# A new order table for a fused attention and two-layer kernel, and 48 casts of its gated layer given to another engine

## The chip, the cores and the metric

The kernel runs on one core of a Trainium2 chip. The core has a matrix engine (TensorE, PE below), a vector engine (VectorE, DVE), a scalar engine (ScalarE, ACT), a third elementwise engine (GpSimd, POOL) and a sync engine (SyncE, SP) that here only issues transfers. Each works through its own queue of instructions in order and waits at semaphores for the others; PE writes its results into PSUM, the others read them there. The metric is the device time of one launch in microseconds, as a median over several runs.

## The reference

Three layers one behind the other. The first is an attention with a state that is corrected at each of 768 steps; the second is gated, with an RMS norm ahead of it; the third has one activation, h·tanh(softplus(h)).

```python
k_n = k / (np.linalg.norm(k, axis=-1, keepdims=True) + 1e-06)   # B=4, H=8, S=768, D=48
for t in range(S):
    kt, vt, bt = (k_n[:, :, t], v[:, :, t], beta[:, :, t, None])
    y[:, :, t] = np.einsum('bhd,bhde->bhe', q[:, :, t], state)
    v_old = np.einsum('bhde,bhd->bhe', state, kt)
    state = state + bt[:, :, :, None] * np.einsum('bhd,bhe->bhde', kt, vt - v_old)
x = np.ascontiguousarray(y.transpose(0, 2, 1, 3)).reshape(B * S, H * D)     # 3072 x 384
xn = x / np.sqrt(np.mean(x * x, axis=-1, keepdims=True) + 1e-06) * rms_g
g = xn @ w_gate                                                            # 384 x 1536
x = (g * (1.0 / (1.0 + np.exp(-g))) * (xn @ w_val)) @ w_out                # 1536 x 384
h = x @ w_in2                                                              # 384 x 2048
out = (h * np.tanh(np.log1p(np.exp(h)))) @ w_out2                          # 2048 x 384
```

## The kernel before

**Numbers in two halves.** All products of the two layers are made from a high half that PE reads at its fast rate and a low half with the rest, in three matmuls (high·high, high·low, low·high). So each operand needs a cast that makes the high half and a subtraction that makes the low one. The weights come as 64-bit numbers and are first put together on DVE, 128x384 at a time, in `value`: L268 (ACT) or L270 (DVE), then L272, L275, L280 and L283 (DVE); after it the high half L305 (ACT) or L307 (DVE) and the low half L308 (DVE or POOL). L357 is the cast of the same kind for the third layer's weights.

**Phase one: attention, with part of the gated layer beside it.** The 768 steps are 12 rows of 64. A row turns its `q` and `k` (transposes L789 on PE, copied out by L790 on ACT), makes the scores `p` (L769 on PE, masked by L779 on DVE into `PT`), the values (L1163, copied by L1168 on ACT into `ve`), the part that comes from the state (L1138), the outputs (L1181, copied by L1189) and the update of the state (L1214 on PE, added by L1219 on DVE). Ahead of that a triangular 64x64 system is inverted for each head and row. The first four rows use a short form of this, the "quick lane": L938 to L1005 on DVE make the blocks `N`, `X` and `A` in 16x16 pieces, and L1023 on PE multiplies them up, with L1028 on DVE (`Zq`) between two of the multiplications. L690 on DVE normalises a row's `kh`. From row 2 on, a first part of the gated layer (two of six blocks of its hidden width) runs beside the rows: up products L421 to L423, SiLU L473, down products L455 to L457, whose sums are copied by L1303 (`par`) on ACT or DVE and stored. L1242, L1245 and L1252 make a row's two halves of the layer's input.

**Phase two** (`phase_b2`, `gated_pairs`) computes the remaining four blocks for 6 pairs of rows. A unit is nine matmuls of 512 columns for `pg`, nine for `pv` (L1461 to L1463, tile `pu` in the profile), and nine down products L1474 to L1476. Between them ACT makes the SiLU `sg` (L1484), DVE multiplies it by `pv` (L1487) and casts the product to its high half `hh` (L1490), and POOL subtracts for the low half `hl` (L1491). A unit's down products are issued two units later (`LG`=2). Beside the units run the conversions of the third layer's weights and, in `forms_of`, sums and halves of the layer's finished output (L1561 on ACT, L1562 on POOL, L1574 on DVE).

**Phase three** is the third layer, almost all matmul.

**What sets the order.** The work is written as Python generators. Two functions decide whose next piece is issued: `plan` takes for each stream a list of due times and always advances the stream with the earliest one, and `merge` shares out by cost. All their numbers stand in one table `P`: `ROW0`, `ROW1`, `QP`, `L`, `K1` to `K4`, `S`, `T`, `G`, `CV` are due times of the first four rows' streams and of the weight conversions; `R0` to `R11` are the order of the steps in each row (`q0 q1` the turning of q, `p` the scores, `r` the residual, `v` the values, `y` the part from the state, `o0 o1` the outputs, `k` the state's update, and so on); `DUE`, `CVS`, `LR`, `C` are amounts and costs for `merge`. The due times order the program text alone; the chip goes by queues and semaphores. Further entries pick an engine: `XDR` and `PDR` say for each row whether L1245 and L1303 are on DVE (1) or ACT (0), `BAV` and `BLV` whether the high half of a weight of the remaining blocks is made on ACT (1) or DVE, and whether its low half is made on DVE (1) or POOL.

Of the kernel before, what the change touches and what calls it, by code (L numbers as in the profile page):

```python
# [19 lines left out]
P = dict(  # L20
    LN0=0.527,
    LNT=(101.823, 0.05),
    FAV=[0, 1, 1, 0, 0, 0],
    XDR=[0, 0, 0, 0, 0, 0, 0, 1, 0, 1, 0, 1],
    PDR=[0, 0, 0, 0, 0, 1, 0, 0, 0, 0, 0, 1],
    BLV=[0, 0, 0, 0, 0, 1, 0, 0, 1, 1, 0, 1],
    BAV=[0, 1, 1, 1, 1, 1, 1, 0, 0, 0, 1, 1],
    CB=[12.0, 12.0],
    PF=[5.192, 30.818, 9.175, 4.627, -31.291],
# [27 lines left out]
    R6="nA q0 q1 S r nB T y v p X Y k o0 c0 c1 g o1".split(),
    R7="r q0 nA q1 S p nB T v y X Y c0 o0 c1 o1 k g".split(),
    R8="r nA q0 S T q1 p X y nB v Y c1 o0 g c0 k o1".split(),
    R9="r nA q0 S q1 nB T p X c1 y v k g Y c0 o0 o1".split(),  # L60
    R10="r q0 q1 p S y X T v o0 Y o1 k".split(),
    R11="S r q0 q1 p T y X Y v o0 k o1".split(),
    DUE=[-20.443, 5.84, 4.881, 10.56, 10.883, 10.311, 10.883, 10.566, 8.191, 10.779, 10.857, 11.898],
    CVS=[-0.332, 18.493, 8.167, -23.236, 9.058, -3.972, 15.147, -22.515, -14.058, -35.503, -28.424, -8.878],
    LR=[-10.2, 25.182, 19.094, 12.02, 16.416, 13.382, 22.451, 16.703, 20.252, 19.685, 56.75, 78.665],
    C={'n': 0.225, 'q': 0.5, 'r': 1.4, 'y': 1.1, 'p': 1.2, 'v': 1.2, 'o': 0.9, 'k': 1.38, 's': 0.168, 'x': 0.595,
        'c': 0.4, 'd': 0.167, 'g': 1.02, 'h': 1.357},
    ROW0=[23.019, 25.696, 30.249, 44.915, 45.626, 49.289, 21.158, 3.409, 52.039, 52.631, 54.162, 59.926, 14.374,
        44.933, 77.944],
    ROW1=[53.942, 35.537, 46.444, 56.274, 50.209, 32.154, 23.865, 62.891, 61.444, 37.535, 36.083, 60.421, 59.815,  # L70
        70.152, 81.857, 92.68, 97.453],
# [1777 lines left out]
```

## Time and profile before

| | |
|---|---|
| median of 3 runs | 1129.47 us (1128.81 to 1129.47) |
| the profiled execution, its time | 1129.23 us |
| the profiled execution, its span | 1127.5 us |
| busy: PE, DVE, ACT, POOL | 1064.6, 826.8, 498.8, 451.1 us |
| mean granted clock of PE | 0.966 of full speed |

The span runs from the first to the last instruction that the profiler recorded; the time of the execution is a little longer. The busy times are those of one execution. An engine's busy time says how much work it has, its idle time says nothing until one sees what waits for it: time is lost only where the chain of work that ends last stands still.

### The profile page before, as it was taken

The numbers are of one execution on the slowest core, as the hardware profiler recorded it, in microseconds if no ns is written. First come the engines' busy times: TensorE is split into PE (matmuls) and PEld (weight loads), VectorE is DVE, ScalarE is ACT, GpSimd is POOL, SyncE is SP. The second block draws the span as 40 slices with busy tenths as digits, with TensorE's granted clock in tenths as the row PEclk, the third lists the DMA queues.
The fourth block names the chain that finished last, engine by engine and source line by source line (L and its number), as shares of the span: only waits on it lengthen the run. The fifth ranks groups of instructions, "written<-read, shape, count | busy, mean of one in ns | idle before, by whom it ended". The sixth has DMA issues, their size and how long they took to land.

```text
span 1127.5 us, 31819 instructions
## 1 busy us (share of the span) xinstructions
PE 1064.6 (94%) x13146; PEld 970.4 (86%) x13146; DVE 826.8 (73%) x1609; ACT 498.8 (44%) x1076; POOL 451.1 (40%) x435
## 2 busy tenths in 40 slices
PE   5778689999999998999999899999999999999997
PEld 5767679999899897888888678889999999999997
DVE  7668898777888889878979983466765656565662
ACT  4475547686657733233333332234433333343333
POOL 2031234443223442466667665534433333333332
PEclk8686799999999999999999999999999999999999
DMA  9033323333236556267769878754735363542621
GB/s 169 7 74 88 101 58 88 87 87 90 56 85 204 181 169 205 75 219 236 244 231 343 277 262 311 267 204 146 249 112 184 94 219 85 165 153 84 207 69 30
DMA packets 178496, 175.18 MB, mean 155 GB/s; under 512 B 84624, under 2 KB 153232, under 8 KB 178352
## 3 DMA queue, kind: packets, MB, share of 16 engines
q1 hardware_dynamic: 169712, 159.00, 46.3%
q10 hardware_dynamic: 8640, 14.16, 3.8%
q8 instruction: 103, 1.69, 0.6%
q14 instruction: 41, 0.34, 0.1%
HBM read 114.53 MB, written 58.59 MB: 154 GB/s over the span
## 4 chain that ended last, share of the span: by engine, by line
PE 79%; DVE 10%; ACT 5%; issue 3%; DMA 2%; SPq 1%; POOL 0%; ACTq 0%; POOLq 0%; DVEq 0%
PE pd L1474 7%; PE pd L1679 6%; PE pd L1678 6%; PE pd L1677 6%; PE ph L1720 5%; PE ph L1721 5%; PE ph L1722 5%; PE pu L1461 4%; PE pu L1463 4%; PE pu L1462 4%; PE pp L769 2%; PE pp L1023 2%; PE pg L421 2%; PE pd L455 2%; PE pp L1181 2%
## 5 line engine op out<-in xcount | busy, mean ns | idle before, releaser
L1667 POOL TENSOR_TENSOR gl<-t,gh 128x512 fp32r<-128x512 f32 x96 | 124.1, 1294 | 244.8 <-ACT gh L1666 201.1
L1729 DVE TENSOR_TENSOR ou<-ou,ph 128x256 f32<-128x256 f32 x210 | 88.4, 421 | 121.8 <-ACT ou L1727 71.9
L1655 ACT ACTIVATE t<-t 128x512 f32<-128x512 f32 x96 | 60.9, 634 | 185.9 <-DVE t L1729 181.0
L1491 POOL TENSOR_TENSOR hl<-sg,hh 128x512 fp32r<-128x512 f32 x48 | 65.8, 1370 | 79.2 <-DVE hh L1490 78.8
L1677 PE MATMUL pd<-wqh,gh 128*128 128x384 f32 x288 | 97.4, 338 | 0.0
L1679 PE MATMUL pd<-wqh,gl 128*128 128x384 f32 x288 | 97.2, 338 | 0.0
L1678 PE MATMUL pd<-wql,gh 128*128 128x384 f32 x288 | 97.2, 338 | 0.0
L483 POOL TENSOR_TENSOR hl<-sg,hh 128x512 fp32r<-128x512 f32 x24 | 34.5, 1437 | 84.9 <-DVE hh L482 50.6
L1487 DVE TENSOR_TENSOR sg<-sg,pu 128x512 f32<-128x512 f32 x48 | 32.7, 681 | 47.4 <-PE pu L1463 32.0
L283 DVE SCALAR_TENSOR_TENSOR t<-raw,t 128x384 int32<-128x384 int32 x68 | 60.6, 892 | 2.4
L1666 ACT CAST gh<-t 128x512 fp32r<-128x512 f32 x96 | 59.5, 621 | 3.9
L1562 POOL TENSOR_TENSOR fx<-xu,fx 128x256 fp32r<-128x256 f32 x60 | 49.9, 839 | 17.4 <-ACT fx L1561 16.4
L1677 PEld LDWEIGHTS pd<-wqh,gh 128*128 128x128 f32 x288 | 54.5, 189 | 0.0
L1678 PEld LDWEIGHTS pd<-wql,gh 128*128 128x128 f32 x288 | 54.4, 189 | 0.0
L1679 PEld LDWEIGHTS pd<-wqh,gl 128*128 128x128 f32 x288 | 54.0, 188 | 0.4 <-POOL gl L1667 0.4
L1484 ACT ACTIVATE sg<-pu 128x512 f32<-128x512 f32 x48 | 28.5, 594 | 49.1 <-PE pu L1463 47.8
L280 DVE SCALAR_TENSOR_TENSOR t<-raw,t 128x384 int32<-128x384 int32 x68 | 46.6, 685 | 1.4
L421 PE MATMUL pg<-XP,wgh 128*128 128x256 f32 x144 | 45.5, 316 | 0.0
L1561 ACT CAST fx<-xu 128x256 fp32r<-128x256 f32 x60 | 23.4, 402 | 49.6 <-DMA xf_d<-fx 27.1
L421 PE MATMUL pv<-XP,wvh 128*128 128x256 f32 x144 | 44.9, 312 | 0.0
L275 DVE TENSOR_SCALAR t<-t 128x384 int32<-128x384 int32 x68 | 42.7, 627 | 2.3
L455 PE MATMUL pd<-hh,woh 128*128 128x256 f32 x132 | 39.8, 301 | 2.3 <-ACT par L1303 2.2
(331 smaller groups left out, 3619.0 us busy)
## 6 DMA issues: line engine op xcount, KB each, us to landing
xf_d<-fx SPq DMA_DIRECT2D x96, 256.0 KB, 3.1
wr<-wi_d SPq DMA_DIRECT2D x120, 192.0 KB, 2.6
XG<-xf_d SPq DMA_DIRECT2D x40, 384.0 KB, 4.5
raw<-in_moe_w_out_dram SPq DMA_DIRECT2D x28, 384.0 KB, 3.9
wi_d<-ws SPq DMA_DIRECT2D x20, 384.0 KB, 3.2
XP<-xf_d SPq DMA_DIRECT2D x20, 384.0 KB, 6.1
raw<-in_moe_w_in_dram SPq DMA_DIRECT2D x16, 384.0 KB, 3.9
wq_d<-ws SPq DMA_DIRECT2D x16, 384.0 KB, 4.1
```

The costliest lines, as they stand in the source:

```text
L283: nc.vector.scalar_tensor_tensor(out=ti, in0=low, scalar=29, in1=ti, op0=ALU.logical_shift_right, op1=ALU.bitwise_or)
L421: nc.tensor.matmul(ps[:, f, :], wh[:, kt, sl], xh[:, kt, :], start=(kt == 0), stop=False)
L455: nc.tensor.matmul(ps, wh[:, f, sl], hh[:, f, :], start=(i + f == 0), stop=False)
L1474: nc.tensor.matmul(ps, w[:, f, cols_of[o]], h, start=first and i == 0, stop=last and i == 2)
L1491: nc.gpsimd.tensor_tensor(out=hl, in0=sg, in1=hh.bitcast(F32), op=ALU.subtract)
L1655: nc.scalar.activation(out=t, in_=t, func=ACTF.Mish)
L1666: nc.scalar.copy(gh, t)
L1667: nc.gpsimd.tensor_tensor(out=gl, in0=t, in1=gh.bitcast(F32), op=ALU.subtract)
L1677: nc.tensor.matmul(ps, gh, wh, start=(f == fs[0]), stop=False)
L1678: nc.tensor.matmul(ps, gh, wl, start=False, stop=False)
L1679: nc.tensor.matmul(ps, gl, wh, start=False, stop=last)
L1729: nc.vector.tensor_tensor(out=at(to), in0=at(a), in1=at(b), op=PLUS[sign])
```

## The change

The table `P` gets new numbers nearly throughout, and three options are added. Two of them (`HC`, which would move the casts of the first part of the gated layer, and `DG`, another way to take diagonal blocks) are zero everywhere and change nothing in the program. The third, `HB`, is 1: the 48 casts of L1490 are issued on ACT. The core of the diff:

```diff
-    XDR=[0, 0, 0, 0, 0, 0, 0, 1, 0, 1, 0, 1],
-    PDR=[0, 0, 0, 0, 0, 1, 0, 0, 0, 0, 0, 1],
-    BLV=[0, 0, 0, 0, 0, 1, 0, 0, 1, 1, 0, 1],
-    BAV=[0, 1, 1, 1, 1, 1, 1, 0, 0, 0, 1, 1],
+    XDR=[0, 0, 0, 0, 0, 0, 0, 0, 0, 1, 0, 1],
+    PDR=[0, 0, 0, 0, 0, 0, 0, 0, 0, 0, 0, 0],
+    BLV=[1, 0, 0, 0, 0, 1, 0, 1, 0, 1, 1, 1],
+    BAV=[0, 1, 1, 1, 1, 1, 1, 0, 1, 0, 0, 1],
...
-    R1="r nA q0 q1 y v p o0 o1 s0 s1 nB k x0 c0 c1 g".split(),
+    R1="r nA q0 q1 p v y o0 nB o1 s1 s0 k x0 c0 c1 g".split(),
...
+    HC=[0] * 24,
+    DG=[0] * 6,
+    HB=1,
...
-                    nc.vector.tensor_copy(hh, sg)
+                    nc.scalar.copy(hh, sg) if P["HB"] else nc.vector.tensor_copy(hh, sg)
                     nc.gpsimd.tensor_tensor(out=hl, in0=sg, in1=hh.bitcast(F32), op=ALU.subtract)
```

In numbers of instructions: PE issues the same matmuls. From DVE go the 48 casts, six products L1245 (row 7) and six copies L1303 (rows 5 and 11); ACT gets the casts, the copies, and six instances of L1252 with two subtractions on POOL in the place of the products. Of the 12 weights of the remaining blocks three have their low half moved from POOL to DVE and one from DVE to POOL, and one high half each is moved from ACT to DVE and from DVE to ACT. On PE the order of phases two and three is unchanged; that of phase one changes in places, of which two are shown. The lines of the changed kernel have numbers that are higher by 6 (L769, L789) or 10 (L1023 and above).

The first place is PE's queue for row 0, at about 20 to 40 us of the profile. `qp` is row 0's q, `kh_185` and `kh_186` are the k of rows 2 and 3, and the matmuls into `p_558` and `p_559` (64 in all, of which the first stand here) are row 0's scores. Before:

```order
L769 MATMUL pp<-kT_189 64x64 x32
L789 MATMUL pp<-ident,qp 128x128 x8
L789 MATMUL pp<-ident,kh_185 128x128 x8
L769 MATMUL pp<-kT_190 64x64 x32
L769 MATMUL p_558<-QT,kT_188 64x64
L769 MATMUL p_559<-QT,kT_188 64x64
...
L789 MATMUL pp<-ident,kh_186 128x128 x8
L769 MATMUL pp<-kT_191 64x64 x32
L662 MATMUL pp<-bnat,sel 128x192 x4
L1023 MATMUL pp<-A_194,N__178 32x32 x64
```

and after, where the scores go to `p_484` and `p_485`:

```order
L775 MATMUL pp<-kT_189 64x64 x32
L795 MATMUL pp<-ident,qp 128x128 x8
L775 MATMUL p_484<-QT,kT_188 64x64
L775 MATMUL p_485<-QT,kT_188 64x64
...
L795 MATMUL pp<-ident,kh_185 128x128 x8
L775 MATMUL pp<-kT_190 64x64 x32
L795 MATMUL pp<-ident,kh_186 128x128 x8
L775 MATMUL pp<-kT_191 64x64 x32
L668 MATMUL pp<-bnat,sel 128x192 x4
L1033 MATMUL pp<-A_194,N__178 32x32 x64
```

The scores (now L775) have moved from behind the transposes and products of `kh_185` to ahead of them.

The second place is PE's queue for row 1, at about 74 to 88 us. The matmuls `pp<-QT,kT_189` are row 1's scores, `pp<-v,A_192` (L1163) its values, `pp<-sx,QT` (L1138) the part from the state, and `pp<-A_194,N__178` (L1023) the first product of the next quick lane. Before:

```order
L789 MATMUL pp<-ident,qp 128x128 x4
L1138 MATMUL pp<-sx,QT 64x48 x32
L1163 MATMUL pp<-v,A_192 64x48 x32
L769 MATMUL pp<-QT,kT_189 64x64 x32
L1239 MATMUL pp<-ident,po 128x128 x3
L789 MATMUL pp<-ident,kh_187 128x128 x8
L1181 MATMUL pp<-ve_196,PT 64x96 x8
L1181 MATMUL pp<-ve_197,PT 64x96 x8
L1214 MATMUL pp<-ve_196,kh_184 64x48 x16
L1214 MATMUL pp<-ve_197,kh_184 64x48 x16
L1023 MATMUL pp<-A_194,N__178 32x32 x64
```

and after:

```order
L795 MATMUL pp<-ident,qp 128x128 x4
L775 MATMUL pp<-QT,kT_189 64x64 x32
L1173 MATMUL pp<-v,A_192 64x48 x32
L1148 MATMUL pp<-sx,QT 64x48 x32
L1191 MATMUL pp<-ve_196,PT 64x96 x8
L795 MATMUL pp<-ident,kh_187 128x128 x8
L1249 MATMUL pp<-ident,po 128x128 x3
L1191 MATMUL pp<-ve_197,PT 64x96 x8
L1224 MATMUL pp<-ve_196,kh_184 64x48 x16
L1224 MATMUL pp<-ve_197,kh_184 64x48 x16
L1033 MATMUL pp<-A_194,N__178 32x32 x64
```

The scores have moved ahead of L1163 and L1138, which have changed places with each other, and the first outputs L1181 (now L1191) stand ahead of the transposes of `kh_187`.

The third place is ACT's queue in phase two, at about 636 to 650 us: `sg<-pu` is a unit's SiLU, `ws<-t` and `t<-raw` are the last and the first step of a weight's conversion, `fx<-xu` is the high half of an output sum. Before:

```order
L357 CAST ws<-t 128x384
L268 ACTIVATE t<-raw 128x384
L1561 CAST fx<-xu 128x256 x2
L1484 ACTIVATE sg<-pu 128x512
L357 CAST ws<-t 128x384
L268 ACTIVATE t<-raw 128x384
L357 CAST ws<-t 128x384
L268 ACTIVATE t<-raw 128x384
L1484 ACTIVATE sg<-pu 128x512
```

and after, in which L1500 is the cast that was L1490 on DVE:

```order
L360 CAST ws<-t 128x384
L271 ACTIVATE t<-raw 128x384
L1571 CAST fx<-xu 128x256 x2
L1494 ACTIVATE sg<-pu 128x512
L360 CAST ws<-t 128x384
L271 ACTIVATE t<-raw 128x384
L1500 CAST hh<-sg 128x512
L360 CAST ws<-t 128x384
L271 ACTIVATE t<-raw 128x384
L1494 ACTIVATE sg<-pu 128x512
L360 CAST ws<-t 128x384
```

Behind each SiLU, with one or two steps of a conversion between, there now stands a cast that reads what DVE has made of that SiLU.

## Rows read from the trace of the kernel before

**Rows 1.** The page of the kernel before: busy time of an engine, and the chain of waits by engine.

```profile
PE 1064.6 (94%) x13146; PEld 970.4 (86%) x13146; DVE 826.8 (73%) x1609; ACT 498.8 (44%) x1076; POOL 451.1 (40%) x435
...
PE 79%; DVE 10%; ACT 5%; issue 3%; DMA 2%; SPq 1%; POOL 0%; ACTq 0%; POOLq 0%; DVEq 0%
```

**Rows 2.** Busy time of each engine by stretch of the span (x instructions), clock, DMA share.

```profile
0.00:150.00 150.00, 107.73 (x3253) 98.17 (x3253) 113.04 (x248) 81.60 (x169) 29.94 (x46) 0.77 0.39 83
125.00:150.00 25.00, 14.36 (x322) 12.92 (x320) 24.26 (x52) 10.52 (x23) 9.32 (x9) 0.84 0.25 73
150.00:420.00 270.00, 264.11 (x5934) 245.64 (x5931) 227.87 (x374) 172.52 (x411) 105.55 (x105) 1.00 0.41 112
590.00:655.00 65.00, 60.95 (x252) 47.70 (x252) 63.55 (x90) 21.71 (x51) 41.98 (x39) 0.97 0.90 310
650.00:654.00 4.00, 4.00 (x13) 3.09 (x12) 3.90 (x8) 0.00 (x0) 1.28 (x1) 0.57 0.93 355
```

**Rows 3.** Timeline of PE, 20 to 45 us: start, duration, instruction, [idle time ended by].

```profile
29.81 1.94 PE L789 MATMUL pp<-ident,kh 128*128 128x128 f32 x8 [7.48 <-issue]
...
35.27 1.93 PE L769 MATMUL p<-QT,kT 64*64 64x64 f32 x64
...
41.89 1.29 PE L1023 MATMUL pp<-A,N__178 32*32 32x32 f32 x128
```

**Rows 4.** PE's waits, 590 to 655 us: us in total, times, longest.

```profile
PE pu L1461 <- DVE sg L1487: 2.2, 3, 1.5
PE pu L1461 <- ACT sg L1484: 1.9, 1, 1.9
```

**Rows 5.** Timeline of DVE, 25 to 45 us.

```profile
26.00 0.93 DVE L690 TENSOR_TENSOR kh<-kh,rn 128x768 f32<-128x768 f32 x1
...
28.76 0.95 DVE L690 TENSOR_TENSOR kh<-kh,rn 128x768 f32<-128x768 f32 x1
...
37.11 1.06 DVE L997 STREAM_TRANSPOSE A<-e 128x512 f32<-128x512 f32 x1
...
38.73 1.09 DVE L1005 STREAM_TRANSPOSE A<-e 128x512 f32<-128x512 f32 x1
43.23 0.69 DVE L1028 TENSOR_TENSOR Zq<-pp,qc 128x512 f32<-128x512 f32 x1 [3.41 <-PE pp L1023]
```

**Rows 6.** Timeline of ACT, 24 to 30 us.

```profile
24.93 1.05 ACT L790 COPY QT<-pp 128x512 f32<-128x512 f32 x2
```

**Rows 7.** Timeline of ACT, around 118 and around 649 us.

```profile
118.36 1.28 ACT L473 ACT_TABLE_LOAD   x1
...
120.15 1.01 ACT L268 ACTIVATE t<-raw 128x384 f32<-128x384 f32 x2
...
648.05 0.51 ACT L357 CAST ws<-t 128x384 fp32r<-128x384 f32 x1 [3.02 <-DVE t L283]
...
648.92 0.57 ACT L1484 ACTIVATE sg<-pu 128x512 f32<-128x512 f32 x1
```

**Rows 8.** Timeline of PE, 73 to 92 us.

```profile
76.90 0.68 PE L1138 MATMUL pp<-sx,QT 64*64 64x48 f32 x32 [0.99 <-ACT QT L790]
...
79.58 1.16 PE L769 MATMUL pp<-QT,kT 64*64 64x64 f32 x62 [0.95 <-ACT ve L1168]
```

**Rows 9.** Timeline of DVE, 79 to 122 us.

```profile
80.77 1.29 DVE L779 TENSOR_TENSOR PT<-pp,mpos 128x512 f32<-128x512 f32 x2 [5.39 <-PE pp L769]
...
120.73 0.36 DVE L272 TENSOR_SCALAR t<-t 128x384 f32<-128x384 f32 x1 [4.48 <-ACT t L268]
```

**Rows 10.** DVE by line, 595 to 655 us: xcount, busy us, mean ns.

```profile
L283 DVE SCALAR_TENSOR_TENSOR t<-raw,t 128x384 int32<-128x384 int32 x13 | 13.5, 1040 | 0.5
...
L1490 DVE CAST hh<-sg 128x512 fp32r<-128x512 f32 x8 | 3.9, 490 | 0.3
```

**Rows 11.** The page's costliest groups: out<-in, xcount, busy us, mean ns.

```profile
L1666 ACT CAST gh<-t 128x512 fp32r<-128x512 f32 x96 | 59.5, 621 | 3.9
```

**Rows 12.** The casts L1490, 580 to 660 us: ns minimum/median/maximum, first and last start.

```profile
L1490 DVE CAST hh<-sg x11: 426/428/743, 584.7 to 659.4; 128x512 fp32r<-128x512 f32 x11
```

More of the change, by code (lines that the diff above doesn't have):

```diff
@@ L33 @@
     TB=4,
-    LANE=17.902,
+    LANE=17.897,
     AFTER=6.2,
-    LD=2.543,
+    LD=2.702,
     CVT=9.0,
@@ L57 @@
[L57 to L71, printed above, removed]
@@ L84 @@
-    T=[8.74, 12.356, 29.899, 32.334],
-    G=[11.07, 18.231, 4.585, -15.646],
+    R4="r nA q0 T q1 p nB S y X v Y c0 o0 k c1 g o1".split(),
+    R5="r nA q0 q1 p T y nB S X v Y c0 c1 o0 k g o1".split(),
+    R6="nA q0 q1 nB S r T y v X p Y k o0 c0 c1 o1 g".split(),
+    R7="r q0 nA q1 S p nB T v y X Y c0 o0 c1 k o1 g".split(),
+    R8="r nA q0 S T q1 p v X y nB Y c1 o0 g c0 k o1".split(),
+    R9="r nA q0 S nB q1 c1 T p X v y g k Y c0 o0 o1".split(),
+    R10="q0 q1 p r S y X T v o0 Y o1 k".split(),
@@ new lines @@
+    R11="S r q0 q1 p v y T X k Y o0 o1".split(),
+    DUE=[-6.851, 5.84, 4.881, 10.56, 10.883, 10.311, 10.883, 10.495, 8.203, 10.605, 10.869, 11.93],
+    CVS=[-0.332, 18.493, 8.167, -24.65, -27.037, -37.657, -19.515, -61.539, -49.205, -70.165, -63.379, -8.878],
+    LR=[-10.2, 21.494, 19.043, 13.937, 16.019, 13.048, 23.207, 16.774, 19.804, 20.824, 55.053, 74.744],
+    C={'n': 0.225, 'q': 0.5, 'r': 1.4, 'y': 1.1, 'p': 1.2, 'v': 1.2, 'o': 0.9, 'k': 1.587, 's': 0.168, 'x': 0.595,
+        'c': 0.4, 'd': 0.167, 'g': 1.02, 'h': 1.764},
@@ new lines @@
+    HC=[0] * 24,
+    DG=[0] * 6,
+    HB=1,
+    ROW0=[23.019, 26.028, 23.493, 44.915, 45.859, 49.073, 21.158, 3.409, 52.039, 51.821, 54.259, 59.926, 31.574,
+        43.397, 76.837],
+    ROW1=[53.942, 35.214, 44.06, 56.274, 52.678, 31.783, 22.846, 58.857, 60.716, 36.807, 34.879, 59.293, 35.217,
+        69.214, 81.129, 91.952, 97.453],
+    QP=[[37.124, 37.449, 35.748, 26.234, 23.907], [46.104, 51.045, 20.325, 47.994, 56.112], [63.368, 49.928, 66.42,
+        69.011, 48.635], [74.927, 88.149, 76.965, 73.06, 70.769]],
@@ L86 @@
+    L=[(19.303, 1.152), (44.964, 1.232)],
+    FF=(81.706, 4.376),
+    CV=[37.876, 19.543, 17.064, 72.572, 60.58, 54.136, 28.254, 62.88, 46.414, 76.003, 58.797, 81.358, 73.271,
[3 rows of a table added]
+    K1=[-29.982, 6.362, -15.835, -17.448],
+    K23=[12.043, 13.762, -6.978, 13.741],
+    K4=[45.886, 48.426, 50.474, 37.537],
+    S=[-2.222, 10.628, 22.942, 22.571, 54.472],
+    T=[8.662, 12.356, 28.463, 30.886],
+    G=[11.07, 16.354, -0.054, -18.915],
     BL=33.889,
@@ L481, in gated @@
                 hl = hp.tile([128, 2, T], F32R, tag="hl", name="hl")
-                nc.vector.tensor_copy(hh, sg)
+                if P["HC"][n * FA + m] if pairs[0] == 0 else 1:
+                    nc.scalar.copy(hh, sg)
+                else:
+                    nc.vector.tensor_copy(hh, sg)
                 nc.gpsimd.tensor_tensor(out=hl, in0=sg, in1=hh.bitcast(F32), op=ALU.subtract)
@@ L791, in turn, with diagonal @@
             done.add(key)
-        def diagonal(dst, A):
+        def diagonal(dst, A, sg):
+            if P["DG"][sg]:
+                nc.scalar.copy(dst, A[:, :, 0:32])
+                for o in (32, 96):
+                    nc.scalar.copy(dst[o:o + 32], A[o:o + 32, :, 32:64])
+                return
             nc.scalar.activation(out=dst, in_=A[:, :, 0:32], func=ACTF.Copy, scale=h0[:, 0:1])
@@ L926, in quick_lane @@
             comp = kp.tile([128, 32, 32], F32, tag="X11", name="compq")
-            diagonal(comp, A)
+            diagonal(comp, A, sg)
             for o in (32, 96):
```

23 lines of the change are left out of this document (6 added, 17 removed), and 6 rows, old and new, of the table CV.

## The prediction

> **What bounds the kernel now.** Three views, from coarse to fine. The page first [rows 1]: TensorE (PE) is busy for 1064.6 of 1127.5 us, and the chain of work that ended last is PE for 79%, DVE for 10%, ACT for 5%. So time is to be had only in the 62.9 us where PE idles, or where its clock is low. The table by stretch shows where that is [rows 2]: of the first 150 us PE is busy 107.73, so 42.3 of the idle time lie there, at a mean granted clock of 0.77; from 150 to 420 it idles 5.9 us of 270, and from 590 to 655 4.05 of 65, which leaves 10.7 for all the rest. There are thus two places: the start, where the attention's chains run from PE to DVE and ACT and back, and the short stretch 590–655, where DVE is busy 63.55 of 65 us. The waits come third. At the start the longest is one of 7.48 us before the transposes L789 [rows 3]; in 590–655 PE waits only for the release of `pu` tiles by L1487 on DVE (2.2 us) and by the SiLU L1484 on ACT (1.9 us) [rows 4].
>
> The profiled execution took 1129.23 us, its span 1127.5, so 1.7 us lie around the span and stay; the median of the three runs is 1129.47, 0.24 above it. I work against 1129.23 and add the 0.24 at the end. A change within 0.2% (2.3 us) I call no difference.
>
> **The first place, around 30 us.** PE stands still for 7.48 us until 29.81, because the next thing in its queue is the transposes of `kh_185`, and the DVE multiplication L690 that normalises it runs at 28.76–29.71, as the second of two [rows 3, 5]. The 64 score matmuls of row 0 (1.93 us at 35.27) stand behind them, although they need only `QT`, which ACT copies from 24.93 to 25.98 [rows 3, 6]. The change puts the scores ahead and both L690 next to each other. The scores then run in the idle time, from 26.0 to 27.9; the second L690 ends at 26.00 + 0.93 + 0.95 = 27.9; the transposes start near 28.0, 1.8 us earlier. PE's way from there to L1023 took 41.89 − 29.81 = 12.1 us, of which 1.9 of scores are gone: L1023 could start at 28.0 + 10.2 = 38.2. It also needs `A` of L997, which ends at 37.11 + 1.06 = 38.17: the same time. What is late next is DVE: its Zq (L1028, 43.23, after 3.41 of idling) follows L1005, which ends at 39.82 [rows 5]; L1023's first group, 1.29 us long, ends earlier, at 39.5. The gain at Zq is 43.23 − 39.82 = 3.4. I take **3.3**, and as the low end 1.8, the earlier start of the transposes alone. Two ACT steps L268, which stood in ACT's idle time at 25.9, now stand before the row's `ve` copies; of their 1.0 us (the pair of [rows 7]) I count **0.3** as lost.
>
> **The second place, around 78 us.** Row 1's scores stand behind two groups of matmuls, L1138 and L1163, and their bulk starts at 79.58 [rows 8]. DVE idles 5.39 us for them before L779, and its whole sequence from L779 to Zq hangs on that [rows 9]. The change issues the scores first. They then start with `QT`, for which L1138 waits until 76.90 now [rows 8]; their 1.16 us end near 78.1, and L779, the first of whose two parts needs half of them, can start at about 77.6: 3.2 us earlier than 80.77. Against the full 3.2 stands that `ve`, L1163 and L1138 now come after the scores, and that the state's update L1219, moved forward on DVE by two instructions, waits for what follows them on PE. I take **2.7**; ends 1.0 and 3.2.
>
> **The third place, 96–121 us.** DVE stands still for 4.48 us until 120.73, waiting for the first step of a weight conversion, L268 on ACT, which is queued behind a table load of 1.28 us and a SiLU [rows 7, 9]. The change puts load and SiLU five ACT instructions earlier, ahead of copies that wait for PE anyway. L268 then comes up to 1.28 us plus the SiLU's time earlier. On the other side a Zq that PE waits for goes behind two conversions on DVE, and PE is given nine matmuls of the gated layer to fill that; about 0.6 of the gain may go. Net **0.7**; ends 0 and 1.5. Sum for the start: 3.3 + 2.7 + 0.7 − 0.3 = **6.4**, between 2.5 and 7.8.
>
> **Rows 2 to 11 of the attention, 150–420.** PE idles 5.9 us in all there, so new orders can gain little. What leaves DVE here (six products L1245, six copies L1303) lands on ACT, and DVE has 270 − 227.87 = 42 us of idle time, ACT 97 [rows 2]; that room hides it on either engine. I take 0, ends −2 and +2 (a third of the idle time either way). Likewise 0 for the weights' low halves that change between POOL and DVE, and the high halves that change between DVE and ACT.
>
> **The gated layer's second part.** 48 casts `hh` leave DVE for ACT. In 590–655 they cost DVE 3.9 us (8 at a mean of 490 ns), and DVE is the engine without room there [rows 2, 10]. PE's waits come because DVE falls behind unit by unit; with 2.0 us of casts gone by the first of the two long waits and 3.4 by the second (4 and 7 casts of 0.49), the waits of 1.5 and 1.9 us [rows 4] have lost their cause, and I leave 0.65 of the 4.05: a gain of 3.4, after which PE itself is the limit there. Right behind the wait of 1.9 us the granted clock in 650–654 is 0.57, so mostly the lower of its two levels, 1.2 GHz [rows 2]; 4 us at 0.57 do the work of 2.3, and 1.7 are lost. If the wait goes the dip may go, but one dip proves no cause: I count 1.0. Together **4.4**, ends 2.0 (DVE's waits go, ACT's stays) and 5.7 (all).
>
> On ACT a cast costs 0.62 us, by L1666 of the same size [rows 11]: 48 × 0.62 = 30 us in all, and in 590–655 8 × 0.62 = 5 us, where ACT is busy 21.71 of 65 [rows 2]. What costs is not the time but the queue. The cast waits for L1487 on DVE, and behind it stand L357, L268, the `fx` casts and the next SiLU. From one unit to the next it is (659.4 − 584.7) / 10 = 7.5 us [rows 12]; the subtraction L1491 behind the cast is needed two units later, so 0.62 − 0.43 = 0.2 us more for it lies under 15 us. The next L268 is held by 0.62 us and what is left of L1487; DVE works longer than that on the conversion before it (one L283 takes 1.04 us there [rows 10], one of four steps). So I count nothing, and make the other answer a rival.
>
> **Sum.** 1129.23 − 6.4 − 4.4 = 1118.4, with 0.24 **1118.7 us**. By the low ends of both terms it is 1125.0, and 2 more for rows 2 to 11; by the high ends 1116.0, and 2 less.
>
> **Rivals.** A: the start pays nothing. DVE is busy 24.26 of 25 us in 125–150 [rows 2]; if that stretch starts no earlier because its conversions wait for ACT or for their weights, all that was won before is given back, and only the cast pays: 1129.5 − 4.4 = 1125.1. For it speaks the wait of 4.48 us for L268; against it, that DVE is idle for 150 − 113 = 37 us at the start, in chains that get shorter.
>
> B: the cast pays nothing, since POOL takes the freed DVE time. The casts there take 428 ns at the median, 490 on the mean and up to 743 [rows 10, 12], so something holds DVE up beside its own work. If POOL's subtraction L1491, now behind ACT, holds up each unit's conversion by 0.49 us more than today, the 3.9 us are spent: 1129.5 − 6.4 = 1123.1. The Trainium skill ("SBUF — State Buffer", section "Who interferes with whom") says why it may: a DVE copy within SBUF, and a DVE step with two SBUF inputs, use one port pair with GpSimd, and whichever comes second is blocked for the whole instruction. By that rule the cast's own conflict goes and the subtraction's merely falls on another DVE step; at its worst that gives 1123.1, where the rows' price gives 1118.7, and no row here separates the two.
>
> C, slower: ACT's queue. The wait of 1.9 us arises because the SiLU at 648.92 stands behind an L357 that had itself waited 3.02 us for DVE's L283 [rows 7]. A cast that waits for DVE is one more link of that kind, in every unit. If each of the 11 units from 585 to 660 stalled PE by 1.9 us, they would lose 20.9 where 4.05 are lost now: 1129.5 − 6.4 + 16.9 = 1140. The result is slower from a mean stall of (4.05 + 6.4 + 2.3) / 11 = 1.2 us per unit. Against it: with the same L357 ahead of the SiLUs today, only one such wait occurs in this stretch.
>
> D: nothing measurable, because rows 2 to 11 give back what the start wins and the cast pays its low end: within 2.3 us of 1129.5.
>
> **Chances.** Both pay as summed (1113 to 1122): 0.52. A 0.17, B 0.12, D 0.11, C and anything else slower 0.08. A and B lie below the 0.2% mark, so faster is 0.52 + 0.17 + 0.12 = 0.81, same 0.11, slower 0.08. The range 1112 to 1126.5 holds the sum with its bounds, A and B: 0.81. The likeliest case alone has 1113 to 1122.
>
> **What would show it.** Right: the wait before L789 near 28 us shrinks from 7.5 to about 2, L1028 at 43.23 moves to about 39.9 and L779 at 80.77 to about 74.6, PE idles about 36 us in the first 150, and in 590–655 PE's waits for `pu` are under 1 us, with no dip of the clock behind them. Wrong in the first step: these places are earlier but the rows at 150 us are not (A). Wrong in the second: DVE is still busy 97% there with a longer L283 (B), or the wait is for ACT's `sg` (C). Wrong as a whole: PE idles more than 8 us in 150–420, where its 264 busy us leave no room for a worse order.

## The result, and the profile after

The changed kernel takes 1117.87 us (median of four runs, 1113.8 to 1118.62) where the one before took 1129.47 beside it: a ratio of 0.9891, with a 95% interval from 0.9871 to 0.9911. In a second comparison, with more runs of the kernel before, it was 0.9899 [0.9885, 0.9914]. That is 11 to 12 us, and 1118.7 us was predicted.

The profiled execution of the changed kernel is the fastest of its four, 1113.8 us with a span of 1112.1. About 2.5 us of what it is ahead of the others was won before anything had been moved (below, the last section), so its rows are read against the repeat (span 1119.4) wherever a difference of that size counts. Line numbers are higher by 3 up to L484, by 6 from there to L796 and by 10 from L805 on; so a weight's high half on ACT, L305, is L308 in the changed kernel, and its low half, L308, is L311. The page first, as in [rows 1], with the moved cast beside it:

```profile
PE 1061.1 (95%) x13146; PEld 969.4 (87%) x13146; DVE 787.8 (71%) x1553; ACT 528.7 (48%) x1136; POOL 451.5 (41%) x433
...
PE 81%; ACT 7%; DVE 5%; issue 3%; SPq 2%; POOL 1%; DMA 1%; ACTq 0%; DVEq 0%; POOLq 0%
...
L1500 ACT CAST hh<-sg 128x512 fp32r<-128x512 f32 x48 | 29.8, 621 | 79.4 <-DVE sg L1497 79.4
```

DVE has lost 39 us of work and ACT has gained 30, of which the cast is 29.8, at 621 ns a piece: the price of [rows 11] to the nanosecond. The chain of waits has half as much of DVE (5% for 10%) and more of ACT (7% for 5%). By stretch, with the columns of [rows 2]; 575 to 645 are the same units as 590 to 655 and a few more:

```profile
0.00:150.00 150.00, 117.14 (x3501) 106.75 (x3502) 122.17 (x264) 86.84 (x183) 34.07 (x50) 0.80 0.39 88
125.00:150.00 25.00, 18.73 (x472) 16.79 (x469) 23.57 (x55) 9.18 (x22) 6.35 (x7) 0.86 0.35 78
150.00:420.00 270.00, 263.66 (x5757) 245.73 (x5757) 224.90 (x368) 173.77 (x415) 102.55 (x101) 1.00 0.42 118
575.00:645.00 70.00, 70.00 (x303) 56.51 (x302) 65.63 (x91) 32.57 (x72) 50.09 (x46) 1.00 0.92 313
```

At the start PE now idles 32.9 us instead of 42.3 (36.5 in the repeat); from 150 to 420 it idles 6.3 instead of 5.9; and in the stretch of phase two it does not idle at all, where it had lost 4.05. In the repeat it still idles 1.3 of the 70 us there, in one wait for ACT's SiLU, at a granted clock of 1.00.

The first place, PE and then DVE, as in [rows 3] and [rows 5]:

```profile
23.62 1.41 PE L775 MATMUL p<-QT,kT 64*64 64x64 f32 x64 [3.18 <-ACT QT L796]
25.98 1.94 PE L795 MATMUL pp<-ident,kh 128*128 128x128 f32 x8 [0.95 <-issue]
...
32.43 1.18 PE L775 MATMUL pp<-kT 64*64 64x64 f32 x64 [0.88 <-ACT kT L796]
...
36.36 1.28 PE L1033 MATMUL pp<-A,N__178 32*32 32x32 f32 x128 [1.26 <-DVE A L1007]
```

```profile
24.10 1.78 DVE L696 TENSOR_TENSOR kh<-kh,rn 128x768 f32<-128x768 f32 x2
...
35.18 1.04 DVE L1007 STREAM_TRANSPOSE A<-e 128x512 f32<-128x512 f32 x1
...
36.77 1.08 DVE L1015 STREAM_TRANSPOSE A<-e 128x512 f32<-128x512 f32 x1
37.75 0.65 DVE L1038 TENSOR_TENSOR Zq<-pp,qc 128x512 f32<-128x512 f32 x1
```

The one wait of 7.48 us has become four smaller ones: 3.18 for `QT` ahead of the scores, 0.95 ahead of the transposes, 0.88 for a `kT` copy and 1.26 for `A` of L1007. Zq (L1038) stands at 37.75, right behind L1015, which is what the prediction named as late next; it had put Zq at 39.9 and row 1's mask at 74.6, and the repeat has them at 40.9 and 75.41. The second and third place on DVE, as in [rows 9]:

```profile
72.14 1.29 DVE L785 TENSOR_TENSOR PT<-pp,mpos 128x512 f32<-128x512 f32 x2 [1.39 <-PE pp L775]
...
79.89 1.02 DVE L1229 TENSOR_TENSOR sx<-sx,pp 128x384 f32<-128x384 f32 x2 [1.15 <-PE pp L1224]
...
81.89 1.08 DVE L1015 STREAM_TRANSPOSE A<-e 128x512 f32<-128x512 f32 x1
82.87 0.64 DVE L1038 TENSOR_TENSOR Zq<-pp,qc 128x512 f32<-128x512 f32 x1
...
110.71 0.36 DVE L275 TENSOR_SCALAR t<-t 128x384 f32<-128x384 f32 x1 [2.84 <-ACT t L271]
```

The wait of 5.39 us ahead of the mask is 1.39 now. But a new one has come in behind it: the state's update L1229 waits 1.15 us for PE, and L1015 and Zq stand behind it. The wait of 4.48 us for L268 is 2.84.

### The profile page after: what moved, and what is told of

Same layout as the page of the kernel before. It is cut to its first block, busy times and chain, and to the rows that moved or that the text cites. A ratio compares the mean times of both kernels' runs of the same rounds, so it can differ in the third digit from the quotient of the medians.

```text
span 1112.1 us, 31764 instructions
## 1 busy us (share of the span) xinstructions
PE 1061.1 (95%) x13146; PEld 969.4 (87%) x13146; DVE 787.8 (71%) x1553; ACT 528.7 (48%) x1136; POOL 451.5 (41%) x433
## 4 chain that ended last, share of the span: by engine, by line
PE 81%; ACT 7%; DVE 5%; issue 3%; SPq 2%; POOL 1%; DMA 1%; ACTq 0%; DVEq 0%; POOLq 0%
PE pd L1484 9%; PE pd L1688 6%; PE pd L1687 6%; PE pd L1689 6%; PE pu L1471 6%; PE pu L1473 6%; PE pu L1472 6%; PE ph L1730 5%; PE ph L1731 5%; PE ph L1732 5%; PE pp L775 2%; PE pd L458 2%; PE pp L1033 2%; PE pg L424 2%; PE pp L1191 1%
## 5 line engine op out<-in xcount | busy, mean ns | idle before, releaser
L1501 POOL TENSOR_TENSOR hl<-sg,hh 128x512 fp32r<-128x512 f32 x48 | 69.3, 1445 | 84.0 <-ACT hh L1500 83.2
L1497 DVE TENSOR_TENSOR sg<-sg,pu 128x512 f32<-128x512 f32 x48 | 32.8, 682 | 68.1 <-PE pu L1473 58.0
L489 POOL TENSOR_TENSOR hl<-sg,hh 128x512 fp32r<-128x512 f32 x24 | 34.1, 1421 | 94.0 <-DVE hh L488 78.8
L1500 ACT CAST hh<-sg 128x512 fp32r<-128x512 f32 x48 | 29.8, 621 | 79.4 <-DVE sg L1497 79.4
L286 DVE SCALAR_TENSOR_TENSOR t<-raw,t 128x384 int32<-128x384 int32 x68 | 58.4, 859 | 2.4
L1687 PEld LDWEIGHTS pd<-wqh,gh 128*128 128x128 f32 x288 | 54.5, 189 | 0.0
L1263 POOL TENSOR_TENSOR XP<-xf,XP 128x384 fp32r<-128x384 f32 x20 | 22.5, 1126 | 65.7 <-ACT xf L1262 65.4
L283 DVE SCALAR_TENSOR_TENSOR t<-raw,t 128x384 int32<-128x384 int32 x68 | 46.4, 683 | 1.3
L424 PE MATMUL pv<-XP,wvh 128*128 128x256 f32 x144 | 45.5, 316 | 0.0
```

The costliest lines, as they stand in the source:

```text
L424: nc.tensor.matmul(ps[:, f, :], wh[:, kt, sl], xh[:, kt, :], start=(kt == 0), stop=False)
L1501: nc.gpsimd.tensor_tensor(out=hl, in0=sg, in1=hh.bitcast(F32), op=ALU.subtract)
L1687: nc.tensor.matmul(ps, gh, wh, start=(f == fs[0]), stop=False)
```

## The experiments

Every kernel was timed beside the kernel before on the same chip; ratios are to it, with 95% intervals. In the traces I use one table throughout: the time between fixed instructions, which leaves out where an execution happened to start. "Zq 1" and "Zq 3" are the first and the third L1028, "mask 3, 4, 12" the L779 of rows 2, 3 and 11, "unit 8" and "unit 18" SiLUs of phase two, "phase 3" the first L1655. The first column is the start of the first L690 of rows 2 and 3; each further column counts from the one ahead of it.

| kernel | L690 | to Zq 1 | to Zq 3 | to mask 3 | to mask 4 | to mask 12 | to unit 8 | to unit 18 | to phase 3 |
|---|---|---|---|---|---|---|---|---|---|
| before | 26.0 | 17.2 | 46.8 | 55.9 | 20.2 | 217.0 | 89.8 | 63.0 | 202.2 |
| cast only | 26.7 | 17.5 | 47.5 | 56.2 | 21.5 | 217.0 | 91.1 | 63.0 | 195.7 |
| row 0 in part | 26.4 | 18.2 | 46.9 | 56.4 | 21.3 | 216.9 | 89.8 | 63.0 | 200.9 |
| row 1 | 25.3 | 17.2 | 46.4 | 56.7 | 21.3 | 217.0 | 90.4 | 63.0 | 201.2 |
| row 0 in full | 26.6 | 14.4 | 47.1 | 56.7 | 21.0 | 217.4 | 89.9 | 62.9 | 202.5 |
| rows 0 and 1 | 26.8 | 14.4 | 47.4 | 56.6 | 21.2 | 217.0 | 89.8 | 62.9 | 202.7 |
| order only | 26.6 | 15.0 | 45.4 | 55.1 | 20.9 | 216.2 | 88.3 | 63.0 | 202.9 |
| the change | 24.1 | 13.6 | 45.1 | 52.1 | 20.9 | 215.7 | 91.9 | 63.2 | 195.2 |
| the change, repeated | 26.6 | 14.2 | 45.5 | 54.0 | 20.9 | 216.4 | 92.0 | 63.2 | 196.8 |
| old engines | 26.2 | 14.3 | 45.3 | 53.7 | 20.9 | 216.0 | 90.8 | 63.0 | 196.1 |
| cast on both | 26.9 | 14.3 | 47.8 | 52.3 | 20.9 | 216.4 | 91.4 | 67.2 | 198.8 |
| first cast on DVE | 25.6 | 14.0 | 47.7 | 54.2 | 20.9 | 216.0 | 88.9 | 62.9 | 196.5 |
| update late | 25.4 | 14.0 | 46.4 | 53.5 | 20.9 | 216.5 | 89.4 | 63.0 | 195.5 |
| update last | 26.2 | 14.3 | 43.5 | 54.5 | 20.9 | 216.0 | 88.9 | 63.0 | 196.3 |

One execution each, so a single entry is worth about 1 us in the first four columns; a column is to be read over the kernels that share an edit. PE's clock is part of that scatter. From Zq 1 to Zq 3 the mean granted clock is 0.78 in the profile of before, 0.73 to 0.74 in those of order only, the change, its repeat and old engines, but 0.63 in "row 1" and 0.62 in "cast on both" and "first cast on DVE", which have the entries of 47.8 and 47.7. Between two single entries of that column 2 us can be the clock's.

**The change, repeated.** No edit.

> The changed kernel once more. Its profiled execution (1113.8 us) lies 4 us under the other three (1117.4 to 1118.6), and in it the fourth load of kh lands 1.9 us earlier than in the execution of before, although nothing ahead of it in the queues has changed. If that is chance, a new profile shows a median near 1118 and a span whose DVE norm L680 of that load starts anywhere from 16 to 19 us. If the change itself makes the start earlier, it starts near 16.5 again.

0.9899 [0.9885, 0.9914], 1120.06 us in the median where before had 1131.28. The norm L680 of the fourth load starts late again, as in the other executions (L690 at 26.6 us and not 24.1): the early start was chance, and the median is the number to explain.

**Cast only.** The kernel before with one line:

```diff
-                    nc.vector.tensor_copy(hh, sg)
+                    nc.scalar.copy(hh, sg)
```

> The kernel before with nothing changed but the 48 casts of the second part on ACT. By the prediction's term it gains 4.4 us: 1125.1, with PE's waits for pu under 1 us around 590 to 655. By rival B (POOL takes the freed DVE time) 1129.5; by rival C (ACT's queue) over 1131. If the profile after is taken at its word, the stretch from 540 to 690 alone gains 6.8 us: 1122.7.

0.9959 [0.9943, 0.9975]: 4.6 us, the prediction's term. PE's waits from 540 to 670 are down to one row:

```profile
PE pu L1461 <- ACT sg L1484: 0.3, 1, 0.3
```

and the clock does not fall behind it. From unit 18 to phase three it is 195.7 us instead of some 202, 6 us less; but up to unit 8 it is 91.1 instead of 90, 1 us more. The term is a difference of two.

**Order only.** The change with the casts on DVE (`HB=0`).

> The changed kernel with the 48 casts back on DVE. If the two terms add up, it has the gain of the order alone, 6.4 by the prediction: 1123.1; if the cast is worth 6.8, about 1124.5. If the cast pays nothing (B) it stands at 1118, if the order pays nothing (A) at 1129.5.

0.9931 [0.9918, 0.9944]: 7.8 us. Order and cast alone add to 0.9890, and both together measured 0.9891 and 0.9899. The terms are additive within the intervals, and of the rivals neither A (the start pays nothing) nor B (the cast pays nothing) holds.

**Old engines.** The change with `XDR`, `PDR`, `BLV` and `BAV` as before.

> The changed kernel with the four lists XDR, PDR, BLV and BAV as before, so that six products, six copies and some halves of weights go back to their old engines. The prediction counts them at nothing, with 2 us either way: 1116 to 1120. In the profile after PE waits 2.7 us for the copies on ACT between 150 and 420, where it waited 1.3 before: if those copies are the cause, this kernel is about 1 us faster than the change, 1117; if they hide DVE's lack of time before 460, it is 1 to 3 us slower.

0.9903 [0.9884, 0.9921]: the same as the change. The moves between engines are worth nothing that shows, which is what the prediction counted them at. (The waits named in the expectation are 2.7 us after and 2.2 before, not 1.3.)

**Cast on both engines.** Each cast is made on DVE and then made again on ACT, into the same tile, so the result is the same and the work is more:

```diff
-                    nc.scalar.copy(hh, sg) if P["HB"] else nc.vector.tensor_copy(hh, sg)
+                    nc.vector.tensor_copy(hh, sg)
+                    nc.scalar.copy(hh, sg)
```

> The changed kernel with each of the 48 casts made twice, first on DVE and then again on ACT into the same tile, so that DVE has its old work and ACT the new as well. If DVE's time is what the move pays with, nothing of its gain is left between 540 and 690 us, and ACT's link stays: the ratio to before is that of the order alone, 0.993, or up to 0.3% above. If it pays because POOL is released by another engine (the port), much of the gain stays: 0.990.

0.9962 [0.9944, 0.998], which is 3.5 us worse than the order alone. PE's waits from 470 to 700, and DVE's casts from 585 to 650:

```profile
PE pu L1471 <- ACT sg L1494: 4.1, 3, 2.0
PE pu L1471 <- DVE sg L1497: 2.2, 3, 1.4
```

```profile
L1500 DVE CAST hh<-sg 128x512 fp32r<-128x512 f32 x9 | 6.2, 688 | 0.3
```

DVE's waits are back to the 2.2 us of [rows 4], to the tenth. So the move pays with DVE's time: with the casts still on DVE nothing of it is left, whichever engine releases POOL. ACT's waits are 4.1 us in three places, where before had 1.9 in one [rows 4] and order only 2.4 in two: a cast on ACT that comes later, because DVE is late, holds up SiLUs. That is rival C, and here it costs. The kernel is a little harder on DVE than the one before, since a cast takes 688 ns there where it took 490, and on ACT than the change, since ACT's cast now waits for DVE's; so its 3.5 us are no price of the move, but that DVE's waits come back in full is clear.

**Row 0 in part.** The kernel before with two due times, which move the scores ahead and put the two L690 together:

```diff
-    ROW0=[23.019, 25.696, 30.249, ...
+    ROW0=[23.019, 25.696, 25.7, ...
-    S=[-2.317, 10.764, 23.854, ...
+    S=[-2.317, 10.764, 22.942, ...
```

> The kernel before with the first place alone: row 0's scores ahead of the transposes of kh of row 2, and the two L690 next to each other; all else as it was, the waiting kT copy too. By the prediction 3.3 us less up to L1028 at 43.23, of which 1.5 rest on the kT copy that is not moved here: 1.8 to 3.3, so 0.997 to 0.9985. If the start pays nothing (A): 1.000.

0.9993 [0.9976, 1.0011], which can't be told from nothing. PE, and then ACT:

```profile
28.33 1.94 PE L789 MATMUL pp<-ident,kh 128*128 128x128 f32 x8 [0.36 <-issue]
...
34.91 1.13 PE L769 MATMUL pp<-kT 64*64 64x64 f32 x32 [3.92 <-ACT kT L790]
...
42.63 1.93 PE L1023 MATMUL pp<-A,N__178 32*32 32x32 f32 x128
```

```profile
33.96 0.41 ACT L970 COPY N__178<-X__179 128x128 f32<-128x128 f32 x1 [3.92 <-DVE X__179 L966]
34.27 0.58 ACT L790 COPY kT<-pp 128x512 f32<-128x512 f32 x1
```

The transposes start 28.33 − 26.4 = 1.9 us behind L690 instead of 3.8, as computed. Then PE waits 3.92 us, because ACT's second `kT` copy is queued behind L970, which waits for DVE until 33.96; and L1023 starts at 42.63, not at 38. The stall had only been passed on. What the scores left behind it, PE still has at L662, which starts 13.3 us behind L690 instead of 14.4; but this execution is at the lower level there, and L662 and L1023 take 2.92 and 1.93 us instead of 1.56 and 1.29. The stretch from 39 to 45 us (granted clock third from the end), before and then here:

```profile
39.00:45.00 6.00, 5.18 (x251) 4.63 (x251) 2.55 (x4) 1.99 (x4) 0.00 (x0) 0.96 0.02 3
```

```profile
39.00:45.00 6.00, 5.56 (x168) 4.87 (x163) 1.69 (x3) 1.40 (x3) 0.00 (x0) 0.50 0.01 3
```

So the 18.2 us to Zq 1 hold a lower clock besides the copy.

**Row 0 in full.** The same with one more due time, `T[2]` from 29.899 to 28.463, which puts both `kT` copies ahead of L970 on ACT.

> The kernel before with the first place in full: row 0's scores ahead, the two L690 next to each other, and on ACT both kT copies ahead of L970. With the scores and L690 alone PE's idle time only moved, to 3.92 us before the second half of the kT products, and L1028 came no earlier. If the copies were the missing part, L1028 now comes 3 us earlier after the same start, ratio about 0.997; if not, 0.999.

Zq 1 comes 14.4 us behind L690, 2.8 less than before and 3.8 less than with the part, of which some is the part's lower clock. The 3.92 us of waiting are gone, so the copies were the missing piece. The time is 0.9989 [0.9979, 0.9998]: 1.2 us, less than half of what was won at Zq.

**Row 1.** The kernel before with `p` ahead of `y` and `v` in `R1`; nothing moves on another engine.

> The kernel before with the second place alone: row 1's scores ahead of L1163 and L1138, nothing moved on another engine. By the prediction up to 2.7 us less, 0.9976; in the changed kernel's profiles L779 comes 3.3 us earlier but the Zq after it only 0.5 to 1.9, because L1219 stands ahead of L1005 on DVE and waits for L1214; with L1219 in its old place the Zq may win the whole 2.7 here. If the start pays nothing (A): 1.000.

0.9988 [0.9973, 1.0004], which can't be told from nothing. PE, then DVE:

```profile
85.38 0.94 PE L1181 MATMUL pp<-ve,PT 128*64 128x96 f32 x16 [1.31 <-ACT po L1189]
86.25 1.15 PE L1214 MATMUL pp<-ve,kh 64*64 64x48 f32 x64
87.33 1.45 PE L1023 MATMUL pp<-A,N__178 32*32 32x32 f32 x128
```

```profile
79.04 1.29 DVE L779 TENSOR_TENSOR PT<-pp,mpos 128x512 f32<-128x512 f32 x2 [3.05 <-PE pp L769]
...
84.67 1.06 DVE L997 STREAM_TRANSPOSE A<-e 128x512 f32<-128x512 f32 x1
...
88.82 0.69 DVE L1028 TENSOR_TENSOR Zq<-pp,qc 128x512 f32<-128x512 f32 x1 [0.35 <-PE pp L1023]
```

The mask starts as soon as the scores allow and `A` of L997 is there at 85.73. But PE comes to L1023 only at 87.33, straight from L1214, with 1.31 us of waiting for an ACT copy ahead of that. What was late next was PE's own queue. This execution is at a lower clock there (0.63 from Zq 1 to Zq 3 for 0.78 before; the scores take 2.03 us and not 1.16), so how much would show at Zq 3 at the same clock is open. Over the twelve runs the clock is the same as before, 0.959 and 0.960 on the mean, so the time is not hidden by it.

**Rows 0 and 1**, both edits together.

> The first place in full and the second one (row 1's scores first, the update L1219 behind L1005 as before) in the kernel before. By the prediction these two are 6.0 of the 6.4 us of the order: 0.9947. By the traces of the changed order, in which 3.0 us are won up to L1028 at 43, 0.6 more up to the one at 90 and 2.3 from there to 150, the two places give 3.5 to 5 us, 0.9955 to 0.997, and the rest of the order's 7.8 lies in the conversions behind them.

0.9974 [0.9963, 0.9986]: 2.9 us of the order's 7.8. In the table the rest lies behind them. From Zq 3 to mask 3 these kernels take 56.6 us, like the kernel before, and the ones with the whole new order 52.1 to 55.1.

**First cast on DVE.** The repeat of the change has this on ACT, and on PE, at phase two's first unit (the profile of the change has the same):

```profile
434.35 0.62 ACT L1500 CAST hh<-sg 128x512 fp32r<-128x512 f32 x1 [4.61 <-DVE sg L1497]
...
436.30 0.93 ACT L308 CAST woh<-t 128x384 fp32r<-128x384 f32 x2 [1.33 <-issue]
...
438.02 0.58 ACT L1494 ACTIVATE sg<-pu 128x512 f32<-128x512 f32 x1
```

```profile
438.65 0.50 PE L1471 MATMUL pu<-XP,wgh 128*128 128x512 f32 x1 [1.93 <-ACT sg L1494]
```

The cast waits 4.61 us for L1497 on DVE. Behind it in ACT's queue stand four transfers that ACT issues (L1441, from 434.48 to 436.26), two L308, two L271 and the next SiLU, and PE waits 1.93 us for that SiLU. The issuing is 1.33 us of the 3 between the cast's end and the SiLU. The edit:

```diff
-                    nc.scalar.copy(hh, sg) if P["HB"] else nc.vector.tensor_copy(hh, sg)
+                    nc.vector.tensor_copy(hh, sg) if j == 0 and (m, f) == units[0] else nc.scalar.copy(hh, sg)
```

> The changed kernel with one cast put back on DVE, that of the first unit of phase two. In the repeat of the change ACT waits 4.61 us for that cast's input while three steps that the next SiLU needs stand behind it, and PE then waits 1.93 us for the SiLU and runs at the lower clock for 3.4 us, worth 1.7. If that link is rival C in one place, this kernel gains 2 to 3.5 us over the change, to about 0.987 of before. If the 1.9 us come from DVE's lateness instead, nothing changes: 0.990.

0.9868 [0.9846, 0.9891]. From mask 12 to unit 8 it is 88.9 us instead of 92.0, and PE's waits from 425 to 445 name DVE alone:

```profile
PE pu L1471 <- DVE sg L1497: 1.9, 2, 1.3
```

**Update late, update last.** To that kernel a due time of row 1's update is added: 35.217 becomes 63 in `ROW1`, and L1229 goes behind L1015 on DVE; with 66 it goes behind Zq, and on PE L1224 behind two of the products L1033.

> The changed kernel with the first unit's cast on DVE, and in row 1 the state's update L1229 on DVE behind L1015 instead of ahead of L1012, where it waits 1.4 to 1.6 us for PE. If that wait is what takes the second place's gain away, Zq L1038 comes 1.1 us earlier against L1007 before it (3.3 us behind L1007's end instead of 4.4), and the ratio goes to about 0.986; if PE's own queue sets Zq, nothing changes: 0.987.

> The same, with the update two steps later still: on PE the product with N and the first one with Zq then stand ahead of L1224, on DVE the update behind Zq. The product with N needs L1007 alone and can start 1.9 us earlier, Zq 2.5 us earlier than in the change; but L1224, 1.2 us of PE, no longer fills the wait for Zq. 0.985 if the quick lane's chain sets the end of the stretch, 0.987 if PE's sum does.

DVE in the repeat of the change, then with the update late, then last:

```profile
80.91 1.07 DVE L1007 STREAM_TRANSPOSE A<-e 128x512 f32<-128x512 f32 x1
...
83.44 1.02 DVE L1229 TENSOR_TENSOR sx<-sx,pp 128x384 f32<-128x384 f32 x2 [1.41 <-PE pp L1224]
...
86.38 0.66 DVE L1038 TENSOR_TENSOR Zq<-pp,qc 128x512 f32<-128x512 f32 x1
```

```profile
81.30 1.07 DVE L1007 STREAM_TRANSPOSE A<-e 128x512 f32<-128x512 f32 x1
...
83.99 0.97 DVE L1229 TENSOR_TENSOR sx<-sx,pp 128x384 f32<-128x384 f32 x2
85.78 0.69 DVE L1038 TENSOR_TENSOR Zq<-pp,qc 128x512 f32<-128x512 f32 x1 [0.81 <-PE pp L1033]
```

```profile
80.41 1.07 DVE L1007 STREAM_TRANSPOSE A<-e 128x512 f32<-128x512 f32 x1
...
83.88 0.69 DVE L1038 TENSOR_TENSOR Zq<-pp,qc 128x512 f32<-128x512 f32 x1 [0.67 <-PE pp L1033]
```

From L1007's end to Zq it is 4.4, 3.4 and 2.4 us: the update was in the way. Counted from Zq 1, though, Zq 3 comes earlier with the update last alone (43.5 for 45.5 in the repeat); with the update late it is 46.4, since L1007 itself comes 1.9 us later in that execution. The times are 0.9873 [0.986, 0.9886] for both: 1116.0 and 1116.4 us where before had 1131.2. Against the first cast alone (0.9868) nothing more shows, so what Zq 3 wins is not passed on whole.

The three kernels with the first cast on DVE stand at 0.987, the change at 0.989 and 0.990. Their intervals overlap that of the repeat by little or just touch it, and that of the first comparison by more; no run timed them beside the change itself. With the 2.5 to 3 us that each of the three traces shows at that place against the change and its repeat I take 2 to 3 us over the change as likely. By the medians they beat both kernels.

## Why the prediction was right, point by point

**The two terms.** 6.4 us for the start and 4.4 for the cast were forecast; the order alone measured 7.8 (6.3 to 9.3 by its interval) and the cast alone 4.6 (2.8 to 6.4). The number, 1118.7, was right because both sums were, and they add. That the sum for the start was right is in part luck: its first two places, 6.0 of the 6.4, gave 2.9 together, and the other 4.9 came from where 0.4 had been counted. (The range was said to hold the sum with its bounds; the low ends with the 2 us of rows 2 to 11 are 1127.0, just above its 1126.5.)

**A term that the sum leaves out: PE's clock at the start.** The prediction prices the clock in 590–655 alone. Each run lists its mean granted clock. On the mean over the runs it is 0.958 to 0.960 for the kernel before in the three comparisons of the experiments, 0.959 to 0.960 for the kernels with one or both of the first two places, and 0.964 to 0.968 for the eight with the whole new order. Between 160 and 1100 us the traces have at most one stretch of 3.4 us at the lower level, which is 0.0015 of such a mean, so the difference lies at the start. Among the 61 runs of the kernel before, those with 0.001 more clock are shorter by 0.30, 0.45 and 0.48 us in the three comparisons. At these rates the 0.008 between before and order only go with 2.4 to 3.9 of the 7.8 us, as an estimate. With the new order PE idles less at the start and has the higher clock; no run separates the two.

**The first place: 3.3 forecast, 3.0 measured at Zq 1** (14.3 on the mean over the ten kernels that have it in full, 17.3 without any of it). But the step "as the low end 1.8, the earlier start of the transposes alone" was wrong. Alone that start shows no gain: the `kT` copy behind L970 takes over the whole stall, and the 1.1 us that PE is still ahead at L662 go in the lower clock of that profile. The sum left the copies out, because 28.0 + 10.2 came to the same 38.2 as L997's end; the 12.1 us in it still held a wait of 1.54 us for that copy, and it did not ask how long the wait becomes when the transposes come 1.8 us earlier and L970 does not. In the profile of before:

```profile
34.36 1.14 PE L769 MATMUL pp<-kT 64*64 64x64 f32 x32 [1.54 <-ACT kT L790]
```

**The second place: 2.7 forecast, nothing that shows alone,** and some 1.0 from Zq 1 to Zq 3 with the rest of the order (46.1 for 47.1 on the mean of six and of four kernels). At the same clock it is more: the four with the order at 0.73 to 0.74 have 45.1 to 45.5, and row 0 in full, at 0.73, has 47.1. The step that failed is "its whole sequence from L779 to Zq hangs on that". Two other things set Zq: PE's queue ahead of L1023 (row 1 alone), and in the change L1229, of which I wrote that it stands against the gain, but put it at 0.5. It takes 1.0 to 2.0 of it: with the update late and last, Zq came 1.0 and 2.0 us nearer to L1007. The time of the kernel did not follow (0.9873 for 0.9868).

**The third place: 0.7 forecast, 2.7 measured** in the column from Zq 3 to mask 3 (53.7 on the mean over the eight kernels with the new order, 56.4 over the six with the old one). I had taken one of DVE's two waits there, the one for L268; it fell from 4.48 to 2.84 us in the change, but is 3.12 in the repeat and 4.74 in order only. The other is for PE ahead of the fourth Zq, in the profile of before:

```profile
99.55 0.69 DVE L1028 TENSOR_TENSOR Zq<-pp,qc 128x512 f32<-128x512 f32 x1 [2.58 <-PE pp L1023]
```

It is filled with conversions, and I had booked that as a loss. It is gone in all eight, though in seven of them DVE waits 1.0 to 2.7 us for a high half on ACT (L308) in its place. How much of the 2.7 each of these makes, and how much the clock, is open: no run isolated them.

**Rows 2 to 11: 0 forecast.** From mask 4 to mask 12 the new order is 0.9 us shorter, within the ±2. The moves between engines: 0 forecast, 0 measured.

**The cast: 4.4 forecast, 4.6 measured, made of 6 us won and 1 to 4 lost.** The stretch from unit 18 to phase three is 6.0 us shorter on the mean (196.0 over the seven kernels with the cast on ACT, 202.1 over the six with it on DVE), just above the high end of 5.7. PE's idle time there falls by 3.7 us, where 3.4 were forecast. The clock's dip is real but not in every execution: of the six with the casts on DVE, all with the wait of 1.9 us, four have it (202.2 to 202.9 us) and two do not (200.9 and 201.2), so it costs 1.5 us where it comes, and 1.0 on the mean, which is what was counted for it. The remaining 1.3 us are not explained.

The step that failed is "I count nothing" for ACT's queue. At the first unit the cast costs 1 us in the old order (91.1 for 89.8 up to unit 8) and 2.5 to 3.7 in the new one (90.8 to 92.0 for 88.3 in order only); that fits the times, by which the cast wins 4.6 us in the old order and 3.3 in the new one (1120.06 for 1123.38). In both, the same things stand between it and the next SiLU: four transfers that ACT issues, two high halves of weights (L305, L308 in the changed kernel) and two L268; the list in the prediction had neither the transfers nor the high halves. PE waits 1.9 to 2.4 us for that SiLU in all five kernels that have this cast on ACT. Behind the wait the change and its repeat are at the lower level for 3.4 us, the other three are not. Four microseconds from that SiLU on, in the repeat and then in cast only:

```profile
438.02:442.02 4.00, 3.37 (x11) 2.72 (x12) 3.79 (x9) 2.13 (x5) 0.97 (x1) 0.76 0.86 315
```

```profile
447.30:451.30 4.00, 3.37 (x15) 2.80 (x16) 3.79 (x9) 2.14 (x5) 0.97 (x1) 1.00 0.97 335
```

The rule I used, that DVE works longer on the conversion before than the next L268 is held, holds from the second unit on, but for one wait of 0.3 to 1.3 us for a SiLU in five of the seven kernels; at the first, DVE's mult comes 5 us behind the SiLU, and what is queued behind the cast is needed at once. In the profile of the change:

```profile
422.52 0.58 ACT L1494 ACTIVATE sg<-pu 128x512 f32<-128x512 f32 x1
428.18 0.62 ACT L1500 CAST hh<-sg 128x512 fp32r<-128x512 f32 x1 [5.08 <-DVE sg L1497]
...
431.86 0.57 ACT L1494 ACTIVATE sg<-pu 128x512 f32<-128x512 f32 x1
```

## What to carry to other kernels

When a stall is to be filled, ask of every queue that feeds the next instruction whether it moves too: moving PE's work and DVE's, and leaving one ACT copy where it was, kept the whole stall, and "what is late next" has one answer for each engine. An instruction moved to an engine with time to spare takes its wait along; look for the one place where its input is late and something urgent stands behind it, and leave that one instance where it was. A sum can be right by terms that are wrong both ways: the experiments on single places cost little and showed that more than half of the order's gain lay at other places than the two argued for. And before a microsecond or two between two profiles is put down to an edit, compare the granted clock of the stretch.
